# Block 0's input fetched in fp32 on another queue and converted on two engines, weights first on GpSimd's queue, one input copy made inside SBUF

## The chip, the cores and the metric

The kernel runs on one core of one Trainium2 chip. The core has five engines with instruction streams of their own: TensorE (PE in the profile, with its weight loads as PEld), VectorE (DVE), ScalarE (ACT), GpSimd (POOL) and SyncE (SP), which computes nothing and issues transfers. Transfers between HBM and the on-chip memory SBUF are issued by an engine as an instruction and then run on 16 shared DMA engines. GpSimd's transfers stand in the profile as the software queue q0, SyncE's as the hardware queue q1; the instructions of the engines themselves are fetched over q8 and q14. In this program only GpSimd's transfers change the type on the way (fp32 in HBM to fp16 in SBUF).

The metric is the time of one execution in device microseconds. The median of three runs of the kernel before is 778.82 us (777.23 to 778.98).

## The reference, cut to what matters

The input `x` has 8 sequences of 4096 tokens with 192 channels in fp32. A lightweight causal convolution with 7 taps comes first: the 192 channels are 8 heads of 24, each head has one set of taps, made by a softmax over its 7 weights. Its result goes through a SwiGLU feed-forward block of width 1536.

```python
w = softmax(weight, axis=-1)                       # 8 heads x 7 taps
x_pad = concat([zeros(B, 6, 192), x], axis=1)
x_unf = x_pad[:, idx, :].reshape(B, S, 7, 8, 24)   # window of 7 tokens
y = einsum('hk,bskhg->bshg', w, x_unf).reshape(B * S, 192)
g   = y @ w_gate                                   # 192 x 1536
val = y @ w_val                                    # 192 x 1536
out = (g * sigmoid(g) * val) @ w_out               # 1536 x 192
```

## The kernel before, in words

The 32,768 tokens are cut into 64 blocks of 512; four blocks form a unit (16 units, two to a sequence). The feed-forward work is a loop of 768 steps, 12 for each block. In a step, `gate_val` computes 128 of the 1536 inner channels for the block's 512 tokens: three pairs of matmuls (line 777), gate on one half of PE's rows and val on the other, side by side; then SiLU on ACT (line 786) and the product on DVE (line 788). Three PSUM banks hold gate and three val. `slot` and `down` (line 803) multiply finished products with `w_out` into accumulators, a part of a block at a time; the result is copied out on ACT and DVE (lines 861, 862) and stored through SyncE's queue (line 865).

Before a block can be stepped through, its convolution result `xc` must lie in SBUF with channels on the partitions. There are three ways.

- Blocks 0 to 3 ("early"). `xe_load` fetches overlapping windows of `x` (52 tokens and their 6 predecessors) into a tile `xe`, windows 0 to 5 on the lower 64 partitions and 6 to 9 on the upper. `early` (line 387) multiplies them with banded matrices `wide`, made from the taps; ACT and DVE copy the result to `tme` (lines 405, 414). Blocks 0 to 2 are turned by PE (`eturn`, lines 445, 450); block 3 goes through HBM (`eout`, `efetch`, lines 421, 431).
- Units 1 and 3. `load_x` fetches windows into `x16`, on 32 partitions for each of two halves; the band convolution `conv_half` (line 476) wants the same data a second time on the next 32 partitions. For unit 3, `dup_x` (line 148) makes that second copy with a transfer inside SBUF. For unit 1, `load_x` is called twice for each half, with `low` 0 and 32, and both copies come from HBM.
- All other units are convolved on ACT, DVE and GpSimd beside the steps.

The order of the work is written out by hand: `seq` ties each instruction to the one before it on its engine, so every engine follows the order in which the program text issues, and an instruction that waits holds all behind it on its engine.

GpSimd's order at the start is: two index patterns (lines 190, 192), the three loads of `xe` for block 0, the pattern `cid` (line 197), the gate and val weights in three parts of three loads each (`load_w`, line 168; part m serves steps 4m to 4m + 3 of a block), with the two loads of `xe` for block 1 between the second and the third part, then three loads of `w_out` (line 178), the loads of `xe` for blocks 2 and 3, the four loads of `x16` for unit 1, four small copies for `band` (line 364) and the first load for a unit convolved beside the steps (line 590). SyncE's order is the tap weights `wraw` (line 90), then nothing until block 0's output store; the round trip of block 3 and the stores of unit 1's convolution (line 512) follow.

The chain of preparation on the engines is: eight matmuls on zeros that keep PE busy (line 878), the softmax of the taps on DVE and ACT, two tiny matmuls (line 301), `tap` and `spread` on DVE (lines 310, 312), four matmuls (line 332), the copies to `wide` on ACT and DVE (line 345), then `early(0)`, `eturn(0)` and step 0. ACT's order there is `eyes`, the exponential, a load of the SiLU table, `warmed` (line 270), and `wide`. `early(1)` is issued behind step 6, `eturn(1)` behind step 8, `early(2)` and `early(3)` behind steps 12 and 19, the two `conv_half` of unit 1 behind steps 25 and 31.

Of the kernel before, what the change touches and what calls it, by code (L numbers as in the profile page):

```python
# [10 lines left out]
def kernel(  # L11
# [9 lines left out]
    nc = tc.nc  # L21
    fp32 = mybir.dt.float32
# [8 lines left out]
    B, S, D = x.shape  # L31
# [3 lines left out]
    P = 128  # L35
    Q = 64
# [3 lines left out]
    TB = P * SUBS  # L40
    NCH = Dff // P
    pad = K - 1
# [5 lines left out]
    EO = 52  # L48
    EG = 5
    ER = ((0, 3), (3, 5))  # L50
# [22 lines left out]
    def seq(i):  # L73

        e = i.ins.engine
        if e in last_on:
            tc.add_manual_dep(i.ins, last_on[e].name, NOSYNC, reason="order")
        last_on[e] = i.ins
        return i

    wpool = ctx.enter_context(tc.tile_pool(name="wts", bufs=1))
# [8 lines left out]
    seq(nc.sync.dma_start(out=wraw, in_=weight))  # L90
    fill = wpool.tile([P, P], fp16, tag="fill", name="fill")
    seq(nc.vector.memset(fill, 0.0))


    def windows(t, p0, t0, size, w0, w1, i0=0, i1=None, at=0, after=None):
        i1 = i1 or (Q if size == EO else size + pad)
        i = seq(
            nc.gpsimd.dma_start(  # L98
                out=t[p0 + i0 : p0 + i1, w0 - at : w1 - at, :],
                in_=bass.AP(  # L100
                    tensor=x_flat.tensor,
                    offset=(t0 + size * w0 - pad + i0) * D,
                    ap=[[D, i1 - i0], [size * D, w1 - w0], [1, D]],
                ),
            )
        )
        if after is not None:
            tc.add_manual_dep(i.ins, after.name, SYNC, reason="load in turn")

    xe = {}  # L110

    def xe_tile(e):
        xe[e] = cpool.tile([P, 6, D], fp16, tag="xe", name="xe", bufs=4)

    def xe_load(e):
        for r, (g0, g1) in enumerate(ER):
            w0, w1 = 2 * g0, 2 * g1
            if e == 0 and r == 0:
                windows(xe[e], 0, 0, EO, 1, w1)
                windows(xe[e], 0, 0, EO, 0, 1, i0=pad, i1=Q - 2)  # L120
            else:
                windows(xe[e], Q * r, e * TB, EO, w0, w1, at=w0)

    x16 = {}

# [3 lines left out]
    def load_x(u, r, after=None, low=0):  # L129
        t, t0, w0, p0 = x16[u], u * UT, 4 * NG * r, Q * r + low  # L130
        w1 = w0 + 4 * NG
        if r == 0 and u % upb == 0:
            seq(nc.gpsimd.memset(t[0:pad, 0, :], 0.0))
            windows(t, p0, t0, CO, 0, 1, i0=pad, after=after)
            windows(t, p0, t0, CO, 1, w1)
        elif r == 1 and u == NU - 1:
            last = (UT - 1) // CO
            seq(nc.gpsimd.memset(t[p0 : p0 + 32, last - w0 :, :], 0.0))
            windows(t, p0, t0, CO, w0, last, at=w0)
            windows(t, p0, t0, CO, last, last + 1, i1=UT - CO * last + pad, at=w0)  # L140
        else:
            windows(t, p0, t0, CO, w0, w1, at=w0, after=after)

    def dup_x(u, queue=None):
        for r in range(2):
            p0 = Q * r
            seq(
                (queue or nc.sync).dma_start(
                    out=x16[u][p0 + 32 : p0 + 64], in_=x16[u][p0 : p0 + 32]
                )  # L150
            )
# [8 lines left out]
    def load_w(m):  # L160
        f0, f1 = WF * m, WF * m + WF
        for half, src, i0, i1, s0 in (
            (0, moe_w_gate, 0, SL, 0),
            (1, moe_w_val, 0, SL - 1, 1),
            (1, moe_w_val, SL - 1, SL, 0),
        ):
            seq(
                nc.gpsimd.dma_start(  # L168
                    out=w16[m][Q * half : Q * half + Q, i0:i1, :],
                    in_=src[Q * s0 : Q * (s0 + i1 - i0), f0:f1].rearrange(  # L170
                        "(s q) f -> q s f", q=Q
                    ),
                )
            )
# [11 lines left out]
    def small(name, shape, dt=fp32):  # L186
        return wpool.tile(shape, dt, tag=name, name=name)
# [3 lines left out]
    jn = small("jn", [P, 4, Q], i32)  # L191
    seq(nc.gpsimd.iota(jn, pattern=[[-16, 4], [1, Q]], base=0, channel_multiplier=0))  # L192
    xe_tile(0)
    seq(nc.vector.memset(xe[0][0:Q, 0, :], 0.0))
    xe_load(0)
    cid = small("cid", [P, P], i32)
    seq(nc.gpsimd.iota(cid, pattern=[[1, P]], base=0, channel_multiplier=0))
    load_w(0)
    load_w(1)
    xe_tile(1)  # L200
    xe_load(1)
    load_w(2)
    for m in range(3):
# [3 lines left out]
    for name, first, rows in (("c01", 0, P), ("c2", P, Q)):  # L207
# [10 lines left out]
        seq(nc.gpsimd.tensor_single_scalar(above[name], which[name], 0, op=ALU.is_ge))  # L218
    xe_tile(2)
    xe_load(2)  # L220
    xe_tile(3)
    xe_load(3)
    x16_tile(1)
    for r in range(2):
        for low in (0, 32):
            load_x(1, r, low=low)

    pq_i = small("pq_i", [P, 1], i32)
    seq(nc.vector.tensor_single_scalar(pq_i, pid, 15, op=ALU.bitwise_and))
# [24 lines left out]
    def make_shift(n):  # L254
        seq(
            nc.vector.tensor_tensor(
                shift[:, n : n + 2],
                jn[:, n : n + 2].unsqueeze(2).to_broadcast([P, 2, 2, Q]),
                both.unsqueeze(2).unsqueeze(3).to_broadcast([P, 2, 2, Q]),
                op=ALU.is_equal,  # L260
            )
        )
# [5 lines left out]
    seq(nc.scalar.activation(wexp[:, 0:K], wraw, AF.Exp, bias=wmax))  # L268
    warmed = small("warmed", [P, 1], fp16)
    seq(nc.scalar.activation(warmed, fill[:, 0:1], AF.Silu))  # L270
    make_shift(2)
    wsum = small("wsum", [H, 1])
    seq(nc.vector.tensor_reduce(wsum, wexp, axis=AX.X, op=ALU.add))
# [23 lines left out]
    def spread_taps():  # L297
        bank = apool.tile([P, TB], fp32, tag="acc0", name="tapbank")
        for a in range(2):
            seq(  # L300
                nc.tensor.matmul(
                    bank[:, a * H : a * H + H],
                    split[:, a].rearrange("h k q -> h (k q)"),
                    eye[0:H, 0:H],
                    start=(a == 0),
                    stop=True,
                    skip_group_check=True,
                )
            )
        seq(nc.vector.tensor_copy(tap, bank[:, 0 : 2 * H]))  # L310
        seq(
            nc.vector.tensor_tensor(
                spread.rearrange("p j a h -> p j (a h)"),
                eyes,
                tap.unsqueeze(1).to_broadcast([P, 16, 2 * H]),
                op=ALU.mult,
            )
        )

    wide = small("wide", [P, 2, H, Q], fp16)  # L320
    band = small("band", [P, H, 32], fp16)
# [564 lines left out]
    acc_banks = (apool, "acc0"), (apool, "acc1")  # L886
    keep_warm(8)
    spread_taps()
    keep_warm(4, 2 * P)
    make_wide()  # L890
# [6 lines left out]
    for n in range(n_steps):  # L897
# [8 lines left out]
        at = (25, 31) if u == 0 else (10, 22)  # L906
# [95 lines left out]
```

## Time and profile before

| | |
|---|---|
| median of three runs | 778.82 us |
| lowest, highest | 777.23, 778.98 us |
| span of the profiled execution, first to last instruction | 776.0 us |
| any other time of that execution | not recorded |
| median less span | 2.8 us |
| PE busy | 767.9 us |
| DVE busy | 687.4 us |
| ACT busy | 607.6 us |
| GpSimd busy | 597.8 us |
| granted TensorE clock, mean | 0.999 |
| first matmul of step 0 | at 8.43 us |
| PE busy in the first 45 us | 41.72 us |
| PE busy in the last 16 us (760 to 776) | 11.65 us |

Times are microseconds from the start of the span. An engine's busy time is the sum over its instructions; matmuls are pipelined, so two that stand beside each other in the trace may overlap. Views of single instructions give the start, the length and the operation, and in brackets the idle time before it on that engine and what ended that idle time; "issue" there means that the profile shows nothing that the engine waited for. The landing time of a transfer counts from its issue.

### The profile page before, as it was taken

What the parts mean: (1) busy time and instruction counts of PE and PEld (TensorE: products, weight loads), DVE (VectorE), ACT (ScalarE), POOL (GpSimd) and SP (SyncE); (2) the same over time, 40 slices, a digit from 0 to 9 for tenths busy, and PEclk for the clock granted to TensorE, in tenths of its full rate; (3) what the DMA queues carried; (4) which work ended last, traced back from release to release, by engine and by line L of the source; (5) the groups of instructions that cost most, each with busy time, mean ns of one, the idle gap of its engine ahead of it and who ended that gap; (6) DMA issues with size and microseconds to landing.
All of it is one profiled execution on the core that took longest, in us unless ns stands there. A gap on an engine that the chain in (4) does not pass through costs nothing.

```text
span 776.0 us, 27834 instructions
## 1 busy us (share of the span) xinstructions
PE 767.9 (99%) x11179; PEld 599.6 (77%) x11179; DVE 687.4 (89%) x1034; ACT 607.6 (78%) x1067; POOL 597.8 (77%) x551
## 2 busy tenths in 40 slices
PE   8999999999999999999999999999999999999997
PEld 5666666668888888888888888888888888887876
DVE  7687998999999999999999999999999999997775
ACT  6576887888878878878888888888888788776664
POOL 9100697799999999999999999999999999992000
PEclk9999999999999999999999999999999999999999
DMA  9949854754534536255353443535445352221211
GB/s 136 186 117 125 170 127 102 166 102 102 114 95 104 103 94 124 65 118 118 84 112 86 103 111 77 115 88 116 93 105 115 77 122 70 70 66 38 70 57 42
DMA packets 143651, 79.31 MB, mean 102 GB/s; under 512 B 89146, under 2 KB 143042, under 8 KB 143042
## 3 DMA queue, kind: packets, MB, share of 16 engines
q1 hardware_dynamic: 130690, 61.58, 34.8%
q0 software_dynamic: 12832, 15.96, 13.5%
q8 instruction: 87, 1.43, 0.8%
q14 instruction: 42, 0.34, 0.1%
HBM read 31.92 MB, written 37.83 MB: 90 GB/s over the span
## 4 chain that ended last, share of the span: by engine, by line
PE 97%; POOL 1%; DMA 1%; DVE 1%; issue 0%; ACT 0%; DVEq 0%; POOLq 0%
PE val L777 41%; PE acc L803 33%; PE gate L777 22%; DMA xe<-in_x_dram 1%; POOL w L168 0%; DVE h L788 0%; POOL xe L98 0%; PE cv L476 0%; PE acc L824 0%; PE cv L387 0%; PE turn L445 0%; ACT sig L786 0%; DVE o_sb L862 0%; ACT o_sb L970 0%; POOL jn L192 0%
## 5 line engine op out<-in xcount | busy, mean ns | idle before, releaser
L786 ACT ACTIVATE sig<-gate 128x512 f16<-128x512 f32 x768 | 448.9, 599 | 154.6 <-PE gate L777 105.3
L788 DVE TENSOR_TENSOR h<-sig,val 128x512 f16<-128x512 f16 x768 | 495.2, 683 | 79.4 <-PE gate L777 45.9
L777 PEld LDWEIGHTS <-w 64*128 64x128 f16 x4608 | 338.9, 110 | 135.2 <-issue 1.9
L777 PE MATMUL gate<-pxc,w 64*128 64x512 f16 x1872 | 438.7, 376 | 0.0
L777 PE MATMUL val<-pxc,w 64*128 64x512 f16 x1872 | 437.6, 376 | 0.5
L803 PE MATMUL acc<-wo,h 64*128 64x192 f16 x6096 | 329.7, 243 | 0.8 <-issue 0.7
L803 PEld LDWEIGHTS <-h 64*128 64x128 f16 x6096 | 300.6, 94 | 28.2 <-ACT sig L786 2.1
L632 POOL TENSOR_TENSOR total<-total,part 128x512 f32<-128x512 f32 x130 | 173.0, 1330 | 45.6 <-DVE total L657 21.8
L657 DVE SCALAR_TENSOR_TENSOR total<-x,both_taps,total 128x512 f32<-128x512 f16 x156 | 166.3, 1066 | 0.0
L647 POOL TENSOR_SCALAR piece<-x,both_taps 128x512 f32<-128x512 f16 x182 | 154.4, 848 | 0.0
L632 POOL TENSOR_TENSOR total<-total,piece 128x512 f32<-128x512 f32 x104 | 141.6, 1362 | 8.7
L777 PE MATMUL gate<-xc,w 64*128 64x512 f16 x432 | 102.1, 377 | 0.0
L777 PE MATMUL val<-xc,w 64*128 64x512 f16 x432 | 101.9, 376 | 0.1
L682 ACT ACTIVATE part<-x,both_taps 128x512 f32<-128x512 f16 x130 | 93.3, 718 | 0.0
L632 POOL TENSOR_TENSOR pxc<-total,piece 128x512 f16<-128x512 f32 x52 | 70.3, 1353 | 4.3
L682 ACT ACTIVATE total<-x,both_taps 128x512 f32<-128x512 f16 x78 | 55.7, 714 | 0.0
L632 POOL TENSOR_TENSOR y<-total,piece 128x512 f16<-128x512 f32 x26 | 33.1, 1273 | 2.2
L862 DVE COPY o_sb<-acc 128x384 f32<-128x384 f32 x63 | 34.5, 547 | 0.0
L861 ACT COPY o_sb<-acc 128x384 f32<-128x384 f32 x63 | 29.6, 471 | 0.1
L98 POOL DMA_DIRECT2D x<-in_x_dram x6 | 5.1, 870 | 24.4 <-ACT sig L786 24.4
L504 POOL COPY tm<-tm 128x1280 f16<-128x1280 f16 x2 | 2.5, 1249 | 19.5 <-DVE tm L493 19.5
L590 POOL DMA_DIRECT2D xs<-in_x_dram x13 | 7.2, 555 | 0.0
(67 smaller groups left out, 74.1 us busy)
## 6 DMA issues: line engine op xcount, KB each, us to landing
out_dram<-o_sb SPq DMA_DIRECT2D x63, 384.0 KB
pxc<-pxc SPq DMA_DIRECT2D x104, 64.0 KB
pxc<-y SPq DMA_DIRECT2D x104, 64.0 KB
xs<-in_x_dram POOLq DMA_DIRECT2D x7, 768.0 KB, 6.7
xs<-in_x_dram POOLq DMA_DIRECT2D x6, 774.0 KB, 6.7
x<-in_x_dram POOLq DMA_DIRECT2D x6, 480.0 KB, 9.4
scr<-tm SPq DMA_DIRECT2D x14, 130.0 KB
x<-x SPq DMA_DIRECT2D x26, 66.0 KB
```

What stands on the lines that cost most here:

```text
L98: nc.gpsimd.dma_start(out=t[p0 + i0 : p0 + i1, w0 - at : w1 - at, :], in_=bass.AP(tensor=x_flat.tensor, offset=(t0 + size * w0 - pad + i0) ...
L590: nc.gpsimd.dma_start(out=flat[skip * D : rows * D].rearrange("(a n) -> a n", n=n), in_=bass.AP(tensor=x_flat.tensor, offset=(u * UT - XP ...
L632: nc.gpsimd.tensor_tensor(job["dst"] if k == K - 1 else total, total, part, op=ALU.add)
L647: nc.gpsimd.tensor_scalar(part, shifted(k), scalar1=job["tap"][:, k : k + 1], scalar2=1.0, op0=ALU.mult, op1=ALU.mult,)
L657: nc.vector.scalar_tensor_tensor(job["total"], shifted(k), job["tap"][:, k : k + 1], job["total"], op0=ALU.mult, op1=ALU.add,)
L682: nc.scalar.activation(part, shifted(k), AF.Copy, scale=job["tap"][:, k : k + 1])
L777: nc.tensor.matmul(o, w16[m][p0 : p0 + Q, k, e::E], xc[b][k][p0 : p0 + Q, 0:TB], start=(k == 0), stop=(k == SL - 1),)
L786: silu[n] = seq(nc.scalar.activation(sg, g, AF.Silu)).ins
L788: seq(nc.vector.tensor_tensor(hj, sg, v, op=ALU.mult))
L803: nc.tensor.matmul(acc[b][bank][:, s, :], hj[p0 : p0 + Q, ts(2 * bank + s, P)], wo16[p0 : p0 + Q, j, :], start=(not second and j == 0 and ...
L861: seq(nc.scalar.copy(o_sb[:, 0:2, :], acc[b][0]))
L862: seq(nc.vector.tensor_copy(o_sb[:, 2:4, :], acc[b][1]))
```

## The change

Four things change, all in the first microseconds.

- Block 0's windows are fetched into a new fp32 tile `xf` by three transfers on SyncE's queue, behind the tap weights. The function `windows` takes a queue for that.
- ACT converts windows 0 to 3 of both halves (128 partitions x 768 elements) into `xe[0]`, between `warmed` and `wide`; DVE converts windows 4 and 5 of the lower half (64 x 384), between `spread` and its half of `wide`. The rows of window 0 that stand before the sequence are zeroed in `xf` instead of `xe[0]`.
- On GpSimd's queue the first part of the weights is the first transfer; `cid` follows it.
- Unit 1's `x16` is loaded once from HBM (two loads instead of four), and `dup_x(1)` makes the second copy with two transfers on SyncE's queue, each of which waits for one of the loads.

```diff
+    xf = wpool.tile([P, 6, D], fp32, tag="xf", name="xf")
+    seq(nc.vector.memset(xf[0:Q, 0, :], 0.0))
+
+    def windows(
+        t, p0, t0, size, w0, w1, i0=0, i1=None, at=0, after=None, queue=None
+    ):
         i1 = i1 or (Q if size == EO else size + pad)
         i = seq(
-            nc.gpsimd.dma_start(
+            (queue or nc.gpsimd).dma_start(
...
     def xe_load(e):
         for r, (g0, g1) in enumerate(ER):
             w0, w1 = 2 * g0, 2 * g1
-            if e == 0 and r == 0:
-                windows(xe[e], 0, 0, EO, 1, w1)
-                windows(xe[e], 0, 0, EO, 0, 1, i0=pad, i1=Q - 2)
-            else:
-                windows(xe[e], Q * r, e * TB, EO, w0, w1, at=w0)
+            windows(xe[e], Q * r, e * TB, EO, w0, w1, at=w0)
...
     xe_tile(0)
-    seq(nc.vector.memset(xe[0][0:Q, 0, :], 0.0))
-    xe_load(0)
+    windows(xf, 0, 0, EO, 1, 2 * ER[0][1], queue=nc.sync)
+    windows(xf, Q, 0, EO, 2 * ER[1][0], 2 * ER[1][1], at=2 * ER[1][0], queue=nc.sync)
+    windows(xf, 0, 0, EO, 0, 1, i0=pad, i1=Q - 2, queue=nc.sync)
+    load_w(0)
     cid = small("cid", [P, P], i32)
     seq(nc.gpsimd.iota(cid, pattern=[[1, P]], base=0, channel_multiplier=0))
-    load_w(0)
     load_w(1)
...
     x16_tile(1)
     for r in range(2):
-        for low in (0, 32):
-            load_x(1, r, low=low)
+        load_x(1, r)
+    dup_x(1)
...
     seq(nc.scalar.activation(warmed, fill[:, 0:1], AF.Silu))
+    seq(nc.scalar.copy(xe[0][:, 0:4, :], xf[:, 0:4, :]))
     make_shift(2)
...
+        seq(nc.vector.tensor_copy(xe[0][0:Q, 4:6, :], xf[0:Q, 4:6, :]))
```

The last added line is the end of `spread_taps`.

More of the change, by code (lines that the diff above doesn't have):

```diff
@@ L92 @@
     seq(nc.vector.memset(fill, 0.0))
-    def windows(t, p0, t0, size, w0, w1, i0=0, i1=None, at=0, after=None):
+    xf = wpool.tile([P, 6, D], fp32, tag="xf", name="xf")
[3 more added lines that the diff above has]
+    ):
         i1 = i1 or (Q if size == EO else size + pad)
         i = seq(
-            nc.gpsimd.dma_start(
+            (queue or nc.gpsimd).dma_start(
                 out=t[p0 + i0 : p0 + i1, w0 - at : w1 - at, :],
```

## The prediction

> **What bounds the kernel now.** I read the page first: its busy shares and the chain that ended last.
>
> ```profile
> PE 767.9 (99%) x11179; PEld 599.6 (77%) x11179; DVE 687.4 (89%) x1034; ACT 607.6 (78%) x1067; POOL 597.8 (77%) x551
> PE 97%; POOL 1%; DMA 1%; DVE 1%; issue 0%; ACT 0%; DVEq 0%; POOLq 0%
> ```
>
> PE (TensorE) is busy 767.9 of 776.0 us and is 97% of the chain, so a change of loading can only give back the 8.1 us in which PE is idle, and the 8 us of preparation in front of the first feed-forward matmul. Next I asked where those idle times lie: the busy time of each engine in three stretches of 45 us.
>
> ```profile
> 0.00:45.00 45.00, 41.72 (x735) 26.85 (x737) 31.23 (x70) 28.89 (x53) 21.95 (x42) 1.00 1.05 148
> 45.00:90.00 45.00, 45.00 (x676) 30.65 (x674) 35.54 (x56) 32.01 (x57) 7.61 (x8) 1.00 0.81 128
> 90.00:135.00 45.00, 45.00 (x696) 30.39 (x694) 41.77 (x63) 36.77 (x67) 38.98 (x35) 1.00 0.61 137
> ```
>
> After the length come PE, PEld, DVE, ACT and POOL, then the granted clock, the DMA share and GB/s. All that the change can reach lies in the first row (3.28 us of PE idle); behind 45 us PE never stops. So I read the start of the chain in order of time, then the weight loads of PE, ACT and PE up to 37 us; start, length and operation stand in each row, and in brackets what ended the idle time before it.
>
> ```profile
> 1.42 2.17 POOL xe L98 x3
> 3.58 0.26 POOL cid L197
> 3.84 3.43 POOL w L168 x6
> 7.27 0.60 POOL xe L98
> 7.87 6.29 DMA xe<-in_x_dram
> 14.21 0.72 PE cv L387 x59
> ```
>
> ```profile
> 8.43 0.11 PEld L777 LDWEIGHTS <-w 64*128 64x128 f16 x1
> 8.88 1.87 PEld L777 LDWEIGHTS <-w 64*128 64x128 f16 x19 [0.35 <-DMA w<-in_moe_w_val_dram]
> 14.21 0.61 PEld L387 LDWEIGHTS <-wide 64*64 64x64 f16 x63 [0.39 <-DMA xe<-in_x_dram]
> 15.67 0.44 PEld L777 LDWEIGHTS <-w 64*128 64x128 f16 x5 [0.24 <-DMA w<-in_moe_w_val_dram]
> 36.68 0.26 PEld L803 LDWEIGHTS <-h 64*128 64x128 f16 x6 [0.95 <-issue]
> ```
>
> ```profile
> 3.95 0.21 ACT L270 ACTIVATE warmed<-fill 128x1 f16<-128x1 f16 x1
> 5.33 0.65 ACT L345 CAST wide<-taps 128x256 f16<-128x256 f32 x2 [1.18 <-PE taps L332]
> ```
>
> ```profile
> 6.08 0.83 PE L387 MATMUL cv<-xe,wide 64*64 64x72 f16 x64 [0.56 <-ACT wide L345]
> ```
>
> To be seen: GpSimd's queue issues block 0's x first (2.17 us), then the weights, then block 1's x, and block 1's convolution waits for the last of these at 14.21. Block 0's own convolution at 6.08 does not wait for x but for `wide`. ACT is empty from 4.16 to 5.33.
>
> **Part 1: weights first on GpSimd's queue.** Three x issues (2.17 us) leave the front of that queue, so all behind them goes out about 2.1 us earlier, until the queue waits for landings. What that removes:
> - First val weights. The first gate matmul stands at 8.43 and its val partner at 8.89; later partners start within 0.02 us of each other. They were issued from 4.38 on and waited for to 8.88; 2.1 us earlier they are there at 6.8. Saved: 0.46 us.
> - Block 1's x. It landed at 14.2; it would land at 12.1. PE wants it after seven steps of three matmul pairs at 0.215 us, 4.5 us after 8.43, so at 12.95. Of the time from 13.72 (the first weight load of this convolution) to 14.21, 0.49 us goes.
> - Third part of the weights: 0.24 us at 15.67 go.
>
> That is 0.46 + 0.49 + 0.24 = 1.19 us. A second account caps it: DVE works through seven products from 10.21 to 14.96 (0.68 each), then the block 1 copies (0.56 and 0.26), which the turning matmuls at 16.43 need. With the first product 0.46 earlier this chain ends at 15.2, so 1.2 us is about what DVE allows as well. I take 1.2; should the later transfers land no sooner, because each is slowed by what now runs beside it, only the first 0.46 remains. The index pattern `cid` (0.27) now stands between the first two parts; DVE wants it at 6.23, and it would be done by 3.6 as before.
>
> **Part 2: block 0's x on SyncE's queue in fp32.** Three issues follow the tap weights' issue (0.75, 0.40 long); at 0.40 each the last is out at 2.35, and nothing else stands on that queue before 29.57 but the copies of part 4. When the data land is not in the trace. Lower end: the tap weights, the only HBM load on this queue, were used 1.38 us after issue began, so 1.95 + 1.38 = 3.3 us. Upper end: 474 KB in fp32 have to arrive; from 2.9 us on, when GpSimd's first transfer moved bytes (1.42 plus 1.5), the weights share the DMA engines. About 150 KB arrive before that, and the other 324 KB at half of the 170 GB/s that the queues carried at their better moments take 3.8 us: 6.7 us. I take 5.0, nearer the middle since the rates in the first 9 us go up to 186 GB/s; both ends stay.
>
> [...]
>
> **Part 3: the conversions.** ACT: 128x768 fp32 to fp16. ACT's copy of 128x256 took 0.403 us, and 128x288 to 128x480 went from 0.401 to 0.562, 0.84 ns an element, so 0.403 + 512 x 0.84 ns = 0.83 us. It stands after `warmed` (ends 4.16) and before `wide`, whose first half (0.375) is needed by 6.05. So it delays PE once x lands after 6.05 - 0.08 - 0.375 - 0.83 = 4.77 us: at 5.0 by 0.25 us, at 3.3 by nothing, at 6.7 by 1.9 us. Behind the waiting copy on ACT stand only `wide` and all of block 0's chain, which moves by the same amount. DVE: 64x384, between 0.28 (128x320 fp16 copy) and 0.56 us (128x384 cast out of PSUM), after `spread` (ends 4.87) and with `pf` (0.15) before its half of `wide` at 5.55: 0 to 0.06 us late, plus what the first landing exceeds 4.87; I take 0.1. The longer memset (192 words for 96) costs under 0.1 us on DVE and nothing on the path: the taps' matmul stands behind the eight warming matmuls, which end at 4.20, while its data were ready at 3.66. If that cover were gone it would cost those 0.1. Sum of parts 2 and 3: +0.35 us, between 0 and 2.0.
>
> **Part 4: second copy of unit 1's x.** GpSimd issues two loads of 480 KB instead of four (0.87 each, 1.7 us less); SyncE issues two copies (0.69 and 1.0 us, the durations of the same copies for another unit). They wait for loads that took 7.5 and 8.4 us and more to land; issued at some 15 and 16 us, they are there at 23 to 25. Behind the waiting copies on SyncE's queue is the first output store (29.57), then block 3's round trip (33.27 to 41.84, wanted at about 51): hidden. The copies are wanted by the convolution at 39.5, 38.3 after the shift. Their own time is unknown: 983 KB at the 225 to 313 GB/s that the hardware queue showed at 34 to 35.5 us are 3.2 to 4.4 us, with landing about 31; if each took as long as the slowest load (13.1 us), 38.5 us. I take 31: no cost.
>
> What goes with the two loads is backlog. Two rows of the DMA answers, each over its own window:
>
> ```profile
> q0 software_dynamic: 1366, 0.52, 200.3%
> q8 instruction: 1, 0.02, 1.6%
> ```
>
> The first is 27 to 30 us: the software queue holds all 16 engines twice over, with block loads that took 7.5 to 13.1 us to land. The second is 33 to 36.5 us: one 16 KB block of PE's instructions, at 34.0 to 34.5. Others came at 18.0 to 18.5 and 26.0 to 26.5, and the next, after PE's stop, already at 37.5 to 38. The stop at 35.96 (0.72 us on PE, ended by "issue") has no wait of the program in it, so I read it as instructions that came late behind that backlog. Two loads less (960 KB at some 170 GB/s, 5.6 us) and an earlier start end the backlog near 30 instead of 36.5 us. I take the stop as gone: -0.7 us; bounds: -0.95 (PEld's figure) and +0.7 (another such stop, the copies taking the place of the loads).
>
> [...]
>
> **Sum.** -1.2 + 0.35 - 0.7 = -1.55 us on a span of 776.0. The page records no other time of its execution; the median of the runs, 778.82, is 2.8 above the span, the fastest, 777.23, 1.2 above. What lies around the span is not touched, so 778.82 - 1.55 = 777.3 us. A change of 0.3% is 2.3 us, about what a measurement of this kernel can tell from no change: the forecast is no change by that bound.
>
> **Rivals.**
> 1. The stop at 36 us remains, or is not caused by the backlog: -0.85, 777.97 us. For it: the cause is inferred. Against: no other stop over 0.6 us stands in the trace's waits of PE behind 37 us, and DMA traffic is lighter there.
> 2. Block 0's x lands late (ends on the other side): past 4.77 us each microsecond costs one. It decides against the change past 4.77 + 1.2 + 0.6 = 6.6 us with the stop gone; at the upper end of 6.7 with the stop kept it gives +0.8, 779.6; slower by 0.3% needs 9 us. For it: the DMA share is already 0.99 at 4 to 6 us. Against: only the 474 KB and the first weights compete then.
> 3. The copies inside SBUF land after 38.3: PE waits for the rest; at 38.5 nothing yet, at 43 us 4.7 - 1.55 = +3.2, 782.0. Against: the rate needed is only 983 KB in 13 us, 76 GB/s.
> 4. All gains at their best, x before 4.77 and PEld's 0.95 us gone, with the two 0.2 us gaps at 10.95 and 12.98 too: -1.2 - 0.95 - 0.4 = -2.55, 776.3 us.
>
> **How the numbers follow.** Forecast 0.45; rival 1 0.21; rival 2 0.12, a third of it past 0.3% with something added; rival 3 0.06; rival 4 0.16. Runs before differ by 1.75 us among themselves, which blurs all cases: faster by over 0.3% has rival 4 nearly whole and some of the forecast, 0.22; slower 0.11; same 0.67. The range takes in rival 4's end and rival 2's upper bound: 776.0 to 779.6.
>
> **What would show it.** Right: no DMA wait of PE at the first val matmul; block 1's convolution starting near 13 us; PE's first convolution at 6.1 to 6.5 us, with ACT's 128x768 copy of 0.83 us ending before 6; no "issue" stop near 35 us; the band convolution without a DMA wait. Wrong: the ACT copy waiting for x past 6 us, new "issue" stops, or a wait for `x` before the band convolution.

## The result, and the profile after

The changed kernel takes 782.15 us, median of five runs (781.53 to 782.93), against 778.65 us (777.21 to 778.98) of the kernel before in its five runs. The ratio is 1.0049, with a 95% interval of 1.0038 to 1.0060: slower by about 3.5 us, where 1.55 us less had been forecast, and outside the range. The profiled execution has a span of 779.5 us for 776.0, 3.5 us more as well, so its trace carries the loss.

The busy shares and the chain of waits on the page of the changed kernel:

```profile
PE 769.8 (99%) x11179; PEld 599.9 (77%) x11179; DVE 693.7 (89%) x1035; ACT 609.3 (78%) x1068; POOL 595.3 (76%) x546
PE 97%; DVE 1%; DMA 1%; ACT 0%; issue 0%; DVEq 0%; ACTq 0%
```

PE still bounds the kernel. Its busy time rose by 1.9 us though its 11179 matmuls are the same, and the idle part of the span rose from 8.1 to 9.7 us. The busy time of the engines in stretches of 45 us (after the length: PE, PEld, DVE, ACT, POOL, granted clock, DMA share, GB/s):

```profile
0.00:45.00 45.00, 40.42 (x705) 26.32 (x707) 28.94 (x67) 27.32 (x50) 17.88 (x37) 0.96 0.87 153
45.00:90.00 45.00, 45.00 (x668) 30.28 (x666) 35.55 (x57) 32.23 (x58) 5.73 (x6) 1.00 0.81 127
```

In the first stretch PE is idle for 4.58 us (3.28 before), it starts 30 matmuls fewer (705 for 735), and the granted clock is 0.96 instead of 1.00. Behind 45 us PE never stops, as before. The chain that ended last, in order of time, names the place (start, length, what; "..." stands for pieces left out):

```profile
2.66 5.32 DMA xf<-in_x_dram
...
8.08 0.83 ACT xe L271
8.91 0.28 ACT wide L348
9.23 1.17 PE cv L390 x42
10.40 0.40 ACT tme L408
10.84 1.78 PE turn L448 x15
```

Block 0's x, issued last at 2.66, has landed at 7.98. ACT converts it, `wide` follows, and block 0's convolution starts at 9.23 instead of 6.08. The turning matmuls then take 1.78 us where they took 1.09. ACT's and SyncE's own rows, with the idle time and its releaser in brackets:

```profile
3.95 0.21 ACT L270 ACTIVATE warmed<-fill 128x1 f16<-128x1 f16 x1
8.08 0.83 ACT L271 CAST xe<-xf 128x768 f16<-128x768 f32 x1 [3.92 <-DMA xf<-in_x_dram]
8.82 0.64 ACT L348 CAST wide<-taps 128x256 f16<-128x256 f32 x2
```

```profile
0.74 0.41 SPq L90 DMA_DIRECT2D wraw<-in_weight_dram  x1
1.21 2.04 SPq L101 DMA_DIRECT2D xf<-in_x_dram  x3
22.97 4.18 SPq L147 DMA_DIRECT2D x<-x  x2
33.06 0.43 SPq L868 DMA_DIRECT2D out_dram<-o_sb  x1
```

ACT stands still for 3.92 us for x. The conversion itself takes the 0.83 us that had been worked out. The three x issues on SyncE took 0.76, 0.61 and 0.59 us, not 0.40 each; their data had landed at 5.33, 7.07 and 7.98. The first output store, at 33.06, is not held up by the copies issued from 22.97 on.

Why the matmuls behind the convolution are slower is seen in PE's windows (length, PE busy with its matmuls, granted clock, DMA share, GB/s). They are cut where the granted clock changes:

```profile
5.94:9.35 3.41, 0.49 (x15) 1.00 1.26 199
9.35:12.76 3.41, 2.92 (x81) 0.50 1.32 200
```

PE had nothing to do from 6.31 to 9.23 (0.49 us busy in a stretch of 3.41 us), and in the next 3.41 us the granted clock is 0.50. Before, it was 1.00 from 3.67 us to the last microsecond. So the late x costs twice: the wait, and then the convolution (1.17 us for 0.83), the turning (1.78 for 1.09) and the first matmuls of step 0 at a clock of 0.50. By the lengths of PE's rows, the convolution and the turning hold 0.97 us of the risen busy time. Another 1.05 us are matmuls on zeros and on the taps, which ran longer because the clock record begins, at full, at 5.94 and not at 3.67; PE had to wait for x behind them, so they cost nothing here.

Each feed-forward step ends with ACT's SiLU, so how far the start of step n's SiLU has moved against the trace of before shows where time is lost or won (us, from the two traces):

| step | before | after | moved | what lies in between |
|---|---|---|---|---|
| 0 | 9.58 | 13.55 | +3.98 | convolution +3.15; from it to the first gate matmul +0.98 (2.35 became 3.33, half clock); from that matmul to the SiLU -0.16 (1.15 became 0.99) |
| 6 | 13.65 | 17.62 | +3.97 | |
| 7 | 15.73 | 19.23 | +3.50 | block 1's x is there: -0.47 |
| 22 | 34.76 | 38.24 | +3.48 | |
| 23 | 37.79 | 40.38 | +2.59 | the stop at 36 us is missing: -0.90 |
| 384 | 394.01 | 396.63 | +2.62 | |
| 767 | 769.42 | 772.78 | +3.37 | +0.75 in many waits of 0.1 to 0.2 us |

### The profile page after: what moved, and what is told of

It reads as the page before. It is cut to its first block, busy times and chain, and to the rows that moved or that the text cites. A ratio compares the mean times of both kernels' runs of the same rounds, so it can differ in the third digit from the quotient of the medians.

```text
span 779.5 us, 27837 instructions
## 1 busy us (share of the span) xinstructions
PE 769.8 (99%) x11179; PEld 599.9 (77%) x11179; DVE 693.7 (89%) x1035; ACT 609.3 (78%) x1068; POOL 595.3 (76%) x546
## 3 DMA queue, kind: packets, MB, share of 16 engines
q8 instruction: 87, 1.43, 0.8%
## 4 chain that ended last, share of the span: by engine, by line
PE 97%; DVE 1%; DMA 1%; ACT 0%; issue 0%; DVEq 0%; ACTq 0%
PE val L780 41%; PE acc L806 32%; PE gate L780 23%; DVE h L791 1%; DMA xf<-in_x_dram 1%; PE turn L448 0%; PE cv L390 0%; PE cv L479 0%; PE acc L827 0%; ACT xe L271 0%; ACT sig L789 0%; ACT o_sb L973 0%; DVE o_sb L865 0%; DVE shift L256 0%; ACT tme L408 0%
## 5 line engine op out<-in xcount | busy, mean ns | idle before, releaser
L660 DVE SCALAR_TENSOR_TENSOR total<-x,both_taps,total 128x512 f32<-128x512 f16 x156 | 174.3, 1117 | 0.0
L635 POOL TENSOR_TENSOR total<-total,piece 128x512 f32<-128x512 f32 x104 | 144.8, 1392 | 8.7
L101 POOL DMA_DIRECT2D x<-in_x_dram x4 | 3.5, 876 | 24.4 <-ACT sig L789 24.4
```

The costliest lines, as they stand in the source:

```text
L101: (queue or nc.gpsimd).dma_start(out=t[p0 + i0 : p0 + i1, w0 - at : w1 - at, :], in_=bass.AP(tensor=x_flat.tensor, offset=(t0 + size * w0 ...
L635: nc.gpsimd.tensor_tensor(job["dst"] if k == K - 1 else total, total, part, op=ALU.add)
L660: nc.vector.scalar_tensor_tensor(job["total"], shifted(k), job["tap"][:, k : k + 1], job["total"], op0=ALU.mult, op1=ALU.add,)
```

## The experiments

Ratios are against runs of the kernel before on the same chip, with 95% intervals. "Step n moved" is the SiLU of step n against the trace of the kernel before that the document shows. The theory after the result: x lands late since the weights move beside it, and the idle PE is then given half the clock. The rivals: the landing is late by the fp32 route itself; ACT's order (conversion ahead of `wide`) holds PE up; the copy inside SBUF costs something further on.

### Weights at the time they had before

```diff
     windows(xf, 0, 0, EO, 0, 1, i0=pad, i1=Q - 2, queue=nc.sync)
+    pause = small("pause", [P, 4, Q], i32)
+    for _ in range(7):
+        seq(nc.gpsimd.iota(pause, pattern=[[-16, 4], [1, Q]], base=0, channel_multiplier=0))
     load_w(0)
```

The changed kernel with seven index patterns ahead of the weights on GpSimd, so that the first weight load is issued at 4.02, near the 3.84 of before.

> The changed kernel with seven index patterns ahead of GpSimd's first weight load (some 2.2 us), so that the weights go out when they did before, while x still comes in fp32 on SyncE's queue. If sharing the engines costs what the held run showed (1.9 us between 6.1 and 8.0): x about half of that earlier, ACT's copy at 7.0 to 7.5 us; step 0 about 0.8 us earlier than in the changed kernel, 781.3. If the fp32 route alone were harmless and the order of the weights the whole cause, x would be there by 5 us and the time 778 to 779. If neither matters: 782.1 and x at 8.

Measured: 778.62 us, ratio 1.0010 (1.0001 to 1.0020). GpSimd's, ACT's and PE's rows:

```profile
1.23 2.84 POOL L198 IOTA pause<- 128x256 int32 x7
4.02 0.84 POOL L167 DMA_DIRECT2D w<-in_moe_w_gate_dram  x1
```

```profile
6.15 0.83 ACT L274 CAST xe<-xf 128x768 f16<-128x768 f32 x1 [1.99 <-DMA xf<-in_x_dram]
```

```profile
7.30 0.73 PE L393 MATMUL cv<-xe,wide 64*64 64x72 f16 x64 [1.38 <-ACT wide L351]
8.56 1.78 PE L451 MATMUL turn<-ident,tme 128*128 128x128 f16 x15 [0.53 <-ACT tme L411]
```

x lands at 5.13, 5.96 and 6.05 and the convolution starts at 7.30, 1.93 us sooner than in the changed kernel. The gain was larger than expected, and the trace has the reason: the first packet of the weights moves at 5.71, when x's last one has ended (5.31), so x has the DMA engines to itself here. With the weights where they were, all else that the change does costs 0.1%; about four fifths of the 0.49% come with the order "weights first". By the traces alone the gain is 1.9 us (step 767 moved +1.50 for +3.37), by the medians 3.0 us: the profiled execution here is the longest of its ten runs, that of the changed kernel the shortest of its five.

### Weights held until x has landed

```diff
-    load_w(0)
+    load_w(0, held)
...
+            for x_in in held:
+                tc.add_manual_dep(i.ins, x_in.name, SYNC, reason="x first")
```

The first weight load waits for all three x transfers (`held` is the list of them).

> The changed kernel with the first weight load held until the three fp32 transfers of block 0's x have landed, so that they have the DMA engines to themselves. If sharing with the weights makes x late: last of the three landed at about 5.3 us instead of 7.98 (issued until 3.25, about 1 us of traffic, 1 us until the landing is known), ACT's copy starting there, block 0's convolution at about 7. Rival (the hardware queue is slow by itself for this pattern): x at 7.5 to 8 as in the changed kernel. The time says little here, since the weights come 4 us later: val weights at about 11.5 us, so step 0 no earlier than in the changed kernel, 782 to 784.

Measured: 781.81 us, 1.0040 (1.0027 to 1.0054). The first packet of the weights moves at 8.28, so x has the DMA engines to itself:

```profile
6.14 0.83 ACT L277 CAST xe<-xf 128x768 f16<-128x768 f32 x1 [1.99 <-DMA xf<-in_x_dram]
```

The landings are 5.09, 5.88 and 6.04, the same as with the weights issued at 4.02. That is 0.7 us later than the 5.3 expected, and well ahead of the rival's 7.5 to 8. So the fp32 route on SyncE's queue takes about 6.05 us in the two runs in which nothing runs beside it, and the weights beside it add 1.9 us. By itself the route is no later than GpSimd's fp16 loads, which landed at 5.79 in the trace before and between 5.77 and 6.36 in the six traces with the old order. The run gained little on the changed kernel, since the clock was at 0.50 for two stretches, from 7.24 to 14.07, and from step 0 to 3 another 0.68 us went (moved +3.12 and +3.80), in which half clock and a wait of 0.73 us for val weights lie together. What it shows is the landing; the time needs both transfers.

### Weights first in the kernel before

```diff
     seq(nc.vector.memset(xe[0][0:Q, 0, :], 0.0))
+    load_w(0)
     xe_load(0)
...
-    load_w(0)
     load_w(1)
```

The order alone: x stays fp16, on GpSimd's queue, and is issued behind the first part of the weights (from 3.40 to 5.31).

> The kernel before with only the order of GpSimd's queue changed: the first part of the weights (three loads), then block 0's x in fp16 as before. x is issued 2 us later, from 3.4 to 5.6 us, and lands behind the weights: by the before's 2.5 to 3.2 us from issue 8.4 us, with the 5 us of later loads 10.5. Block 0's convolution at 8.6 to 10.6 instead of 6.1, the clock halved after the wait, step 0 +3.5 to +5.5 us, 781.5 to 783.5. If the order of x and weights did not matter because all share the engines anyway: 778.5.

Measured: 779.42 us, 1.0022 (1.0013 to 1.0031).

```profile
7.75 0.96 PE L387 MATMUL cv<-xe,wide 64*64 64x72 f16 x64 [1.77 <-DMA xe<-in_x_dram]
9.24 1.78 PE L445 MATMUL turn<-ident,tme 128*128 128x128 f16 x15 [0.53 <-ACT tme L405]
```

The direction is right and the size was overestimated: the convolution waits for x until 7.75 instead of 6.08, and the clock is 0.50 from 8.66 to 12.07. Step 0 moved +2.77. The stop at 36 us is absent here too, although unit 1's x is loaded four times as before, and step 23 has moved only +1.39.

### ACT's conversion behind `wide`

```diff
-    seq(nc.scalar.copy(xe[0][:, 0:4, :], xf[:, 0:4, :]))
     make_shift(2)
...
+        seq(nc.scalar.copy(xe[0][:, 0:4, :], xf[:, 0:4, :]))
```

The same copy is issued behind ACT's half of `wide`.

> The changed kernel with ACT's conversion moved behind its two copies to `wide`. If the order on ACT costs what stands behind the waiting conversion, `wide` is done before 7 us and block 0's convolution starts at 8.9 to 9.0 us, right behind the conversion, instead of 9.23: 0.3 us earlier. If the landing of x at 8 us is all, the same start within 0.1 us. Either way far above the kernel before, ratio 1.004 to 1.005.

Measured: 780.29 us, 1.0039 (1.0025 to 1.0053).

```profile
5.74 0.65 ACT L347 CAST wide<-taps 128x256 f16<-128x256 f32 x2 [1.44 <-PE taps L334]
8.30 0.83 ACT L354 CAST xe<-xf 128x768 f16<-128x768 f32 x1 [1.92 <-DMA xf<-in_x_dram]
```

`wide` is ready at 6.39, and the convolution still starts at 9.19, behind the conversion. From x's landing (8.21) to the convolution it is 0.98 us, in the changed kernel 1.25, so ACT's order is worth 0.27 us, about the 0.28 that the first copy of `wide` takes, and no more. The landing sets the start.

### PE kept busy while it waits

```diff
     make_wide()
+    keep_warm(12)
     early(0, (gate_bank, gate_bank, val_bank))
```

Twelve more matmuls on zeros in the changed kernel, between the taps and block 0's convolution.

> The changed kernel with 12 more matmuls on zeros between the taps' matmuls and block 0's convolution, which fill 2.6 of the 3.2 us in which PE waits. x is as late as before. If the halved clock at 9.35 to 12.76 us follows from PE's idle time: no halved clock there, block 0's convolution and turning 1.0 us shorter, 781.1 against 782.15. Rival (the clock's drop has another cause, or falls elsewhere in the first 20 us): same time, 782.15.

Measured: 780.67 us, 1.0029 (1.0018 to 1.0039).

```profile
9.29 0.73 PE L390 MATMUL cv<-xe,wide 64*64 64x72 f16 x64
10.54 1.08 PE L448 MATMUL turn<-ident,tme 128*128 128x128 f16 x15 [0.53 <-ACT tme L408]
```

```profile
6.79:10.20 3.41, 3.23 (x76) 1.00 1.34 193
```

x lands as late as in the changed kernel (8.03), the clock stays at 1.00, and the turning takes 1.08 us again. Step 0 moved +3.02 instead of +3.98, step 767 +2.40 instead of +3.37. Half the clock is thus worth 0.96 us of the loss in the profiled execution, the shortest of the changed kernel's five; by the two ratios it is about 1.6 us, whose intervals just touch.

### The copy inside SBUF alone

```diff
     for r in range(2):
-        for low in (0, 32):
-            load_x(1, r, low=low)
+        load_x(1, r)
+    dup_x(1)
```

The kernel before with part 4 of the change alone; run twice, on two chips.

> The kernel before with only the second copy of unit 1's x made inside SBUF. My reading (the stop of 0.9 us before step 23 comes from the backlog of the software queue): no stop near 36 us, all steps from 23 on 0.9 us earlier, median 777.8 against 778.65. Rival (the stop is not caused by the backlog, or moves elsewhere): the stop stays, 778.6.

> The copy alone once more. The stop before step 23 is missing again. If its 0.9 us are given back later (1.35 us between steps 48 and 767 in the first profile), the same loss shows here and the ratio is 1.000; if that loss was chance, the steps behind 48 keep their distance within 0.4 us and the median lies 0.5 to 0.9 us below the kernel before.

Measured: 778.27 us, 0.9997 (0.9988 to 1.0006), and 777.25 us, 0.9995 (0.9986 to 1.0004): no difference that can be told. In both traces PE runs past step 22 without the stop (from step 22 to 23 it is 2.18 and 2.13 us, 3.03 before; neighbouring steps of the kind take 2.13). In the second one:

```profile
34.36 1.63 PEld L803 LDWEIGHTS <-h 64*128 64x128 f16 x36
35.98 1.71 PEld L777 LDWEIGHTS <-w 64*128 64x128 f16 x18
```

The 36 weight loads that were split by 0.95 us of "issue" are in one row. By the medians the copies neither cost nor gain, though a gain of 0.9 us had been expected, and of the 0.9 us little reaches the end: at step 767 the first execution has moved +0.72 (its clock record begins, at full, only at 5.96, step 0 +0.70, and then again 1.35 us were lost behind step 48), the second -0.38.

### The change without the copy

The edit above, undone in the changed kernel.

> The changed kernel with both copies of unit 1's x loaded from HBM again. If the backlog makes the stop, it is back, at about 36 + 3.5 us, and the time rises by 0.9 us to 783.0; if the stop went for another reason (the later start), the time stays at 782.15. Step 0 as in the changed kernel, first SiLU at 13.55 us.

Measured: 781.25 us, 1.0037 (1.0023 to 1.0051). The four loads from HBM are back, and the stop is not:

```profile
38.26 1.63 PEld L806 LDWEIGHTS <-h 64*128 64x128 f16 x36
```

The time, expected at 783.0 by the backlog, can't be told from the changed kernel's (the intervals overlap). So the missing stop is not the copy's doing. The 16 KB block of instructions (one of the 87 of q8, 1.43 MB together) to which the stop was put down was fetched at 34.33 in the trace before and later still here, at 35.65, but PE comes to step 22 3.9 us later.

### The copy, with the small gap in front of block 0's convolution filled or widened

```diff
     make_wide()
+    keep_warm(2)
     early(0, (gate_bank, gate_bank, val_bank))
```

```diff
-    keep_warm(8)
+    keep_warm(7)
     spread_taps()
-    keep_warm(4, 2 * P)
+    keep_warm(3, 2 * P)
```

Both on the kernel before with the copy.

> The copy alone, with two matmuls on zeros in the gap of 0.56 us in which PE waits for `wide` before block 0's convolution. If a fall of the clock to half in the first 13 us, seen in one of three profiles with the old route of x, follows from such gaps, it no longer falls: no halved stretch in the profile and a narrower spread, median 0.3 to 0.6 us below the kernel before. If the clock does not mind gaps of this size: as the copy alone, ratio 0.9997.

> The copy alone, with seven instead of eight and three instead of four matmuls on zeros around the tap matmuls. At half speed these stand 0.4 us (4.13 to 4.52 us) and 0.2 us in the way of the tap matmuls, whose data are ready at 3.66 and 5.26. If so: 0.4 to 0.6 us earlier at step 0 in executions whose clock starts late, median 777.8 against 778.27 of the copy alone; if fewer of them delay the clock's start: 778.3 or more.

Measured: 777.72 us, 1.0000 (0.9992 to 1.0009), and 777.45 us, 1.0000 (0.9990 to 1.0009). In the first the clock was never halved, and the stop was there in spite of the copy:

```profile
36.20 0.34 PEld L803 LDWEIGHTS <-h 64*128 64x128 f16 x8 [0.94 <-issue]
```

The second has half the clock from 7.46 to 10.88, and step 0 moved +0.96 for the +0.19 of the copy alone. Neither brings a version that beats the kernel before.

### Both kernels again

The kernel before and the changed kernel, unedited, once more.

> The kernel before once more, unchanged, to see what differs between its own executions: its first profile had full matmul speed from 3.8 us on, while four of the five other profiles of this study came to it between 5.9 and 6.8 us. If that early start of the clock is chance, this profile shows the later start, step 0's SiLU at about 10.3 instead of 9.58 us, and the stop before step 23 again (2.1 us added there against the 0.65 us of its neighbours) if the stop belongs to the kernel; ratio 1.000. If the stop is chance too, it is missing here, and then the copy alone gains nothing.

> The changed kernel once more, unchanged. x known to have landed at 7.8 to 8.3 us again, a halved clock of 3.41 us in the first 14 us again, and the steps 3.5 to 4.5 us late at step 0, 0.5 less from step 7 on, 0.9 less from step 23 on. Open: the 0.8 us that it lost between steps 384 and 624; chance would show another figure here, between -0.4 and +0.8, a property of the kernel the same 0.8.

Measured: 777.58 us, 1.0001 (0.9992 to 1.0010), and 781.97 us, 1.0052 (1.0038 to 1.0066). The loss repeats. The kernel before had its stop again, longer (1.74 us of "issue"). The changed kernel's x landed at 8.11, and this time half the clock lasted two stretches:

```profile
5.80:9.22 3.42, 0.45 (x4) 1.00 1.25 202
9.22:12.63 3.41, 2.77 (x79) 0.50 1.36 200
12.63:16.05 3.42, 3.42 (x18) 0.50 1.24 200
```

Step 0 moved +4.68, step 7 +5.08. So the price of the lowered clock varies from one execution to the next, about 1 us here and over 2 us there.

### The runs side by side

Times are us from the start of the span; a dash stands where the fp32 tile isn't used.

| kernel | ratio | x landed | first convolution | clock at 0.50 | step 0 moved | step 767 moved |
|---|---|---|---|---|---|---|
| changed | 1.0049 | 7.98 | 9.23 | 9.35 to 12.76 | +3.98 | +3.37 |
| changed, again | 1.0052 | 8.11 | 9.36 | 9.22 to 16.05 | +4.68 | +4.93 |
| without the copy | 1.0037 | 8.25 | 9.51 | 10.36 to 13.78 | +4.38 | +3.75 |
| `wide` first | 1.0039 | 8.21 | 9.19 | 8.30 to 15.13 | +4.48 | +4.81 |
| kept busy | 1.0029 | 8.03 | 9.29 | none | +3.02 | +2.40 |
| weights held | 1.0040 | 6.04 | 7.30 | 7.24 to 14.07 | +3.12 | +3.76 |
| weights as before | 1.0010 | 6.05 | 7.30 | 8.48 to 11.89 | +2.20 | +1.50 |
| weights first, alone | 1.0022 | - | 7.75 | 8.66 to 12.07 | +2.77 | +1.06 |
| copy alone, first | 0.9997 | - | 6.89 | none | +0.70 | +0.72 |
| copy alone, second | 0.9995 | - | 6.38 | none | +0.19 | -0.38 |
| before, again | 1.0001 | - | 6.38 | none | +0.19 | +0.16 |

## Why the prediction was wrong

**The step that failed** is part 2, the landing of block 0's x: 5.0 us taken, 6.7 as the upper end, 7.98 measured. The 5.0 was taken near the middle of two bounds and not worked out; without any weights beside it x lands at 6.04, and the weights add the other 1.9 us. The issues were taken as 0.40 us each from the tap weights' row; they take 0.76, 0.61 and 0.59, so the last is out at 3.25 and not 2.35. The upper end was closer, but it counted the movement of bytes only. For these it gave 6.7, and x's last packet ends at 6.92; the landing is known 1.06 us after that, a term that the sum doesn't have. The two parts of that 6.7 were off in opposite directions. About a third of x was to be there at 2.9 us, when the weights start; x's first packet moves only at 2.75, and when the first packet of the weights moves, at 3.68, a quarter of x has come. The rest was to come at 85 GB/s and came at 114, though the hardware queue nearly stood still from 4.25 to 4.9 us while the first gate weights moved; with the weights held it came at 191. The shares of the two queues in the first 9 us, of the changed kernel and of the one in which the weights wait for x (packets, MB, share of the time of 16 engines):

```profile
q0 software_dynamic: 906, 0.80, 56.1%
q1 hardware_dynamic: 694, 0.49, 22.0%
```

```profile
q1 hardware_dynamic: 694, 0.49, 23.2%
q0 software_dynamic: 35, 0.04, 4.9%
```

The same 694 packets of the hardware queue bring x and the tap weights; 906 packets of the software queue stand in these 9 us in the one and 35, all behind x, in the other, and x lands at 7.98 or at 6.04.

So a second queue gave x no DMA capacity of its own here: beside the weights it came at 114 GB/s, without them at 191.

**What held of part 2 and 3** is the condition worked out for them. "Past 4.77 us each microsecond costs one": 7.98 - 4.77 = 3.21, and the convolution moved by 3.15. ACT's copy takes 0.83 us as computed. The longer memset (0.22 us) stands on no path.

**A term was missing.** Nothing in the sum priced what idle PE does to the clock. Half the clock cost 0.98 us from the convolution to the first gate matmul, and 0.96 by the run that kept PE busy. With it, parts 2 and 3 come to 3.15 + 0.98 = +4.13 us instead of +0.35.

**Part 1**, -1.2 forecast, gave next to nothing. The wait of 0.35 us at the first val matmul became one of 0.16 at step 0's third, and block 1's convolution no longer waits for x:

```profile
13.15 1.44 PEld L780 LDWEIGHTS <-w 64*128 64x128 f16 x15 [0.16 <-DMA w<-in_moe_w_val_dram]
17.69 0.63 PEld L390 LDWEIGHTS <-wide 64*64 64x64 f16 x64 [0.41 <-issue]
```

That looks like the predicted 0.49 us for block 1. But step 7 comes 0.47 us nearer with the weights as before as well (+2.24 to +1.77), and so it does in the kernel before run again (+0.18 to -0.29), where x of block 1 had landed in time. That wait differs from one execution to the next, and the one of the trace before was not the old order's price. Nor is there much at the val matmuls: from the first gate matmul to step 0's SiLU it takes 1.15 us in the trace before, 1.06 in the kernel before run again and 1.05 in the changed kernel with PE kept busy, all at full clock. The third term, 0.24 us at 15.67, moved the steps by 0.04 (+3.50 at step 8, +3.46 at step 12). So the earlier weights gained 0.1 us or so, and they are the cause of x's late landing.

**Part 4**, -0.7 forecast: the stop is gone (-0.90 by the steps), as predicted, and not for the reason given, so that this term came true by luck. It is gone without the copy, too, when PE comes to step 22 later by 2.3 us (weights first, alone) or 3.9 us, and it can be there with the copy. That it is late instructions fits the runs: the end of the stop stands 2.35, 2.31, 2.26 and 2.29 us after the block's fetch in the four traces that have it (before 34.33 to 36.68, again 34.87 to 37.18, gap filled 33.94 to 36.20, less warming 34.75 to 37.04, a short one whose row names DVE; with the weights held, a trace of one, 0.2 us, ends 2.50 after its fetch at 36.82), and in the trace before the stop begins 1.2 us after the start of step 22's SiLU (35.96 less 34.76). In the changed kernel the block was fetched at 34.23, and by the same distance PE would want it at about 39.4, an estimate. What sets the time of the fetch was not settled: with the copy it lies between 32.54 and 34.75, without it, in kernels with an undelayed start, at 34.33 and 34.87. The copies themselves were hidden, as forecast.

**The late part**, +0.75 us from step 384 to 767, was in no term. It comes in waits of 0.1 to 0.2 us, one pair of steps in a unit. The changed kernel run again lost 0.73 us between steps 384 and 624, as before (0.80), which by its expectation speaks for the kernel and against chance. Behind step 48 all eleven traces of kernels with the fp32 route or the copy lost between 0.50 and 1.35 us; the two others, the kernel before run again and the weights first alone, won about 0.33. So the fp32 route and the copy may each cost something here that the medians of the copy alone don't show. The lost time stands in PE's rows as idle time ended by "issue" (of the waits over 0.12 us of PE's weight loads, 2.86 us in the changed kernel for 2.20 before). No run tells its cause; it stays open.

The measured sum: +4.13 - 0.16 (val) - 0.47 (block 1) - 0.90 (stop) + 0.75 (late), with 0.17 us of small differences, makes the +3.5 us of the span. Rival 2, x late, was the right one; the price of its tail was short by the clock. Its deciding point of 6.6 us rests on the gains of parts 1 and 4, of which the medians show none, so no run supports it.

## What to carry to other kernels

A load on which the start of the chain depends has to be first on the DMA engines, not only first on a queue of its own: here the weights that moved beside it cost it 1.9 us. For a landing, add the issue times of such a load and the time between its last packet and the release of the waiting engine (0.7 to 1.1 us here) to the time of the bytes. And price every new gap of PE near the start twice, once as wait (3.15 us here) and once as matmuls at half clock (0.96 to 0.98 us in the profiled execution), or fill it.

## What the runs showed of the hardware

**The granted clock in the 14 profiled executions.** The clock record begins, at full clock, at a time that differs from one execution to the next, between 3.67 us (kernel before) and 6.95 us (change without the copy). In the first 16 us eight executions show a clock of 0.50, five of them for 3.41 us and three for 6.83 us. The tables give PE's busy time in the stretch of 3.41 us ahead of the fall, and in the first 3.41 us of the record where there was none, then in the first stretch at 0.50, each with the clock measured in the stretch behind it:

| first stretch of the record, at full clock: PE busy, us | clock behind it |
|---|---|
| 0.45 (changed, again), 0.49 (changed), 0.73 (without the copy), 1.03 (`wide` first), 1.59 (weights as before), 1.59 (weights first, alone), 1.72 (weights held), 2.19 (less warming) | 0.50 |
| 2.32 (before, again), 2.33 (copy alone, second), 2.35 (copy alone, first), 2.63 (before), 2.86 (gap filled), 3.23 (kept busy) | 1.00 |

| first stretch at 0.50: PE busy, us | clock behind it |
|---|---|
| 2.03 (`wide` first), 2.49 (weights held), 2.77 (changed, again) | 0.50 |
| 2.88 (weights first, alone), 2.92 (changed), 3.02 (without the copy), 3.33 (weights as before), 3.42 (less warming) | 1.00 |

The copy with less warming, and the stop near 36 us in the kernel before run again:

```profile
4.05:7.46 3.41, 2.19 (x76) 1.00 1.09 136
7.46:10.88 3.42, 3.42 (x25) 0.50 1.17 167
```

```profile
34.99:38.40 3.41, 1.90 (x34) 1.00 0.64 189
38.40:41.81 3.41, 3.41 (x76) 1.00 0.02 6
```

In the first, PE was busy for 2.19 us, the longest of its gaps was 0.56 us, and the clock fell. In the second PE was busy for less, 1.90 us, and the clock stayed full. In the kernel before, PE was busy for 2.67 us of the 3.41 us ahead of the record's beginning, with matmuls at half the rate as told below, and full clock stands behind it; behind the 2.77 us in the table it does not. Busy time alone, as the profile models it, therefore gives no limit; whether the kind of matmul in the stretch counts (convolution and turning in the first, feed-forward work in the second) was not tested.

**Matmuls ahead of the clock record.** In the kernel before, whose record begins at 3.67 us, the matmuls of 512 columns on zeros start every 0.40 to 0.43 us from 1.00 to 3.53. Those of 256 columns start every 0.11 to 0.12 us there (4.26 to 4.60, within the record), and every 0.18 to 0.22 us in the changed kernel (4.66 to 5.27, ahead of its record's beginning at 5.94). The profile's windows print a clock of 1.00 in all these places, since nothing of the clock is recorded ahead of 3.67 and 5.94.

**Landing after the last packet.** With the weights beside it, 1.06 us pass from the end of x's last packet (6.92) to its landing (7.98), and 0.94 to 1.03 in the four other traces of this kind; with nothing beside it, 0.74 (5.30 to 6.04 and 5.31 to 6.05).
